# An FFT mix and a gated product on one core: split of the middle tiles behind two copies, one cast exempt from the hold, longer planned scalings, another order in the first batch

## The chip, the cores and the metric

The kernel runs on one core of a Trainium2 chip. The core has a matrix engine (TensorE, PE), a vector engine (VectorE, DVE), a scalar engine (ScalarE, ACT), a general engine (GpSimd, POOL) and a sync engine (SyncE, SP) that here only issues DMAs. Each works through its own instructions in the order in which the program wrote them, and waits on semaphores for the others. The metric is the device time of one execution in microseconds (us).

## The reference

```python
Xr, Xi = rfft(x, axis=1)                  # x: 8 x 3072 x 256, real
Yr = Xr @ w_r - Xi @ w_i + b_r            # complex linear layer, 256 x 256
Yi = Xr @ w_i + Xi @ w_r + b_i
Yr = sign(Yr) * max(abs(Yr) - 0.01, 0)    # soft shrinkage, Yi the same
y  = irfft(Yr + 1j * Yi, n=3072, axis=1)
out = (y @ w_a) * (y @ w_b) @ w_out       # w_a, w_b: 256 x 1536, w_out: 1536 x 256
```

All of it is float32. The kernel gets that from TensorE with three matmuls for each product: both operands are split in a high and a low part (`h` and `l` in the names), and high x low, high x high and low x high are summed in PSUM. Each split costs a cast (the high part) and a subtraction (the low one).

## The kernel before

**The stages.** The transform of a sequence (a batch, b, of 8) is done in pieces: `fdft` (a small network of adds on POOL and scalings on ACT over a buffer `fd`), f1 (a DFT matmul into `gst`, stored to DRAM as g_d, for the first batches), f2 (a middle DFT of one of 12 tiles u, whose result is split into `sx`), f3 (the complex linear layer and the shrinkage on `zy`, `zc`), i1 (back, into `dst`, stored as d_d), and `idft` (a network of adds on POOL and scalings on ACT over a buffer `wk`), which leaves `y`. y is split into `ych`, `ycl` by yr_split, after sums and differences of its parts (yr_sums).

**The loop.** The second half of the work, w_a, w_b and w_out, runs in 384 steps: 32 pairs p (four quarters q of each batch) times 12 column blocks j. A step (`step`, from L1484) issues seven products of three matmul groups each, by a scheme that saves products through sums. PSUM banks X (bank 3 and 4 in turn), ya (bank 5) and yb (bank 6) hold them. Three times a step ACT copies a bank to SBUF, `s` (L1492, function `take`): s1 after run 0, s2 after run 2, s5 after run 3. Run 2 needs s1 done, run 5 needs s2 and run 4 needs s5, since they go on in the same banks. At the step's end DVE adds and multiplies in yb, ACT casts the result to the high part `g` (L1554), and DVE subtracts for the low part; only then is yb free for run 3 of the next step. The products with w_out (`proj`) read g.

**The slots.** Twice a step, `slot()` takes a task from a list: one f1, f2, f3, i1 or part of the inverse transform of the next batch, so that the transform of batch b + 1 lies between the products of batch b. The list of a pair has 24 slots; `extra(work, n, f)` hangs f on slot n. Filler matmuls (`busy`) stand in front of the loop and keep PE going.

**The planner.** Class `Order` decides where in each engine's program an instruction stands. It holds a planned time for PE and the time until which each other engine is taken, and charges an instruction a fixed time and one for each element (`COST`). A chain of dependent operations is either urgent (its first operations go out by a heap as soon as their planned start is reached), or lazy (it goes out when its engine is planned to be free), or spare (lazier still). `od.hold` is a time: a lazy operation of ACT that would end later than it is not written yet, so that the next copy `s` isn't behind it. `od.need` and `od.vacate` force a chain out at once.

**What the change touches.** The g cast of a step is the first lazy operation after two urgent ones (`urgent=2`, L1554). The split of a middle tile (L945 to L977) is a chain of six operations: cast sx, copy xs, two on DVE, cast sx, one on POOL, of which four are urgent. The scalings are in idft (L1249) and fdft (L1337). `near_move` (L804) moves batch 0's g at the start and loads the first raw weights.

Of the kernel before, what the change touches and what calls it, by code (L numbers as in the profile page):

```python
# [12 lines left out]
F32 = mybir.dt.float32  # L13
# [4 lines left out]
B, S, D, DFF = 8, 3072, 256, 1536  # L18
# [4 lines left out]
M1, G = 24, 5  # L23
# [260 lines left out]
RING = 9  # L284
AHEAD = 1
LATE = 3
# [5 lines left out]
class Order:  # L292
# [34 lines left out]

    def chain(self, *ops, urgent=0, spare=False, after=0.0, hop=None):

        c = {"ops": deque(ops), "left": len(ops), "n": len(ops), "times": [(max(self.pe + self.FROM, after), None)], "urgent": urgent, "hop": self.HOP if hop is None else hop}
        if urgent:
            self._push(c)
        else:
            (self.spare if spare else self.lazy).append(c)
        return c
# [20 lines left out]
    def _held(self, c):  # L358

        if self.hold is None:  # L360
            return False
        e, t = self._choose(c)
        return e == "A" and t > self.hold
# [79 lines left out]
def fft_mix_glu_kernel(ctx: ExitStack, tc: tile.TileContext, x, w_r, w_i, b_r, b_i, w_a, w_b, w_out, c1f, vf, m2, t2, c3, b1, m2b, mf, vb, out):  # L443
# [360 lines left out]
    def near_move():  # L804
        g = state["g"]
        near_load(0, nc.sync.dma_start)
        near_load(1, nc.scalar.dma_start)
        for k in range(2):
            for i in range(2):
                r0 = 4 * (2 * k + i)  # L810
                dma = nc.scalar if k and i else nc.gpsimd
                dma.dma_start(gt[0, k][0][4 * NEAR :, i], g[r0 : r0 + 4])
        for h in range(2):
            n0 = NEAR + 4 * h
            nc.sync.dma_start(g_d[0][16:, n0 * D : (n0 + 4) * D], g[16:, 4 * h : 4 * h + 4].rearrange("p n d -> p (n d)"))
            if h == 0:
                state["wab_load"](1)
        raw = state["raw0"] = state["tmp"].tile([P, 2, 2 * FC], U32, tag="raw", name="wraw", bufs=3)
        for dh in range(2):
            nc.gpsimd.dma_start(raw[:, dh ^ 1], words[0][dh * P : (dh + 1) * P, : 2 * FC])  # L820
# [70 lines left out]
    def f2(b, u):  # L891
# [60 lines left out]
        else:  # L952
# [24 lines left out]
            ops[2:2] = [("G", 10, lambda e: nc.gpsimd.tensor_copy(both3[:, :, 0], xs_[:, :, 0]))]  # L977
        c = od.chain(*ops, urgent=4 if u else 1)
        od.reads(bk, c, 2 if u else len(ops) - 1)
# [240 lines left out]
    def idft(b, q, wait=False):  # L1220
# [25 lines left out]
        def scale(o, x, f):  # L1246
            n = size(*o[1:])
            o, x = at(*o), at(*x)
            ops.append(("A", n, lambda e: nc.scalar.mul(o, x, f)))  # L1249

# [59 lines left out]
    def fdft(b, q):  # L1310
# [23 lines left out]
        def scale(o, x, f):  # L1334
            n = size(*o[1:])
            o, x = at(*o), at(*x)
            ops.append(("A", n, lambda e: nc.scalar.mul(o, x, f)))  # L1337

# [9 lines left out]
    def yr_sums(p):  # L1348
        g = "GV" if p < NPAIR else "G"
        a11, a12, a21, a22 = yr["y"]  # L1350
# [20 lines left out]
    def yr_split(p, k, urgent=0):  # L1371
# [7 lines left out]
        l = state["ring"].tile([P, W], F32R, tag="ycl", name="ycl")  # L1379
        e = "V" if p == 0 else "GV" if p < NPAIR else "G"  # L1380
        ops = split(W, s, wide(h[:, :]), wide(l[:, :]), e)
# [92 lines left out]
    def step(n, nxt):  # L1474
# [46 lines left out]
        od.need(c1_)  # L1521
        od.hold = None
        run(2, X)
# [22 lines left out]
        if n:  # L1546
# [8 lines left out]
            ("V", W, lambda e: tt(e, l1, Y, h1.bitcast(F32), ALU.subtract)),  # L1555
            urgent=2,
        )
        od.reads(yb, c, 0)
# [9 lines left out]
    def first_mid_tasks():  # L1568
        ts = [lambda: f2(0, 0)]
        for u in range(14):  # L1570
# [8 lines left out]
            if u + 2 < 12:  # L1579
                ts.append(lambda u=u: f2(0, u + 2))  # L1580
        return ts

# [28 lines left out]
    with tc.manual_schedule():  # L1611
# [23 lines left out]
        ts[0] = after(ts[0], lambda: [od.put(xs[0, 0][2]), state.pop("start_weights")()])  # L1635
        ts[5] = after(ts[5], lambda: rest.append(split_mix()))

# [9 lines left out]
        ts[-3] = after(ts[-3], lambda: od.put(zs_done[11]))  # L1647
        ts[-2] = after(ts[-2], lambda: [od.put(rest[0]), busy(5, *unread), rows()])
        ts[-9] = after(ts[-9], matrices)
# [5 lines left out]
        have(DFF // FC - 1)  # L1655
        busy(20, *unread)
        for t in f1_tasks(1)[:AHEAD]:
# [46 lines left out]
        for b in range(B):  # L1704
            for q in range(NPAIR):
# [9 lines left out]
                if b == q == 0:  # L1715
# [8 lines left out]
                    extra(work, len(work) - 1, lambda: [mid_load(1, u) for u in range(2)])  # L1724
                    work.append(lambda: f2(1, 0))
                    mids = deque([None, None, *mid_tasks(1, 0)])
                elif b == 0 and q < 3:
                    n = 14 if q == 1 else 10
                    work = [mids.popleft() for _ in range(n)] + fin
                    work += [mids.popleft() for _ in range(20 - n)]  # L1730
                    for n, k in ((11, 1),) if q == 1 else ((3, 2), (19, 3)):
                        extra(work, n, lambda k=k: fdft(2, k))
                elif b + 1 < B:
# [3 lines left out]
                    if q < 3:  # L1737
                        if b + 2 < B:
                            extra(work, 13, lambda b=b, q=q: fdft(b + 2, q + 1))
                    else:  # L1740
                        extra(work, len(work) - 1, lambda b=b: idft(b + 1, 0, True))
                        if b + 2 < B:
                            extra(work, 13, lambda b=b: ahead(b + 2))
                            if b + 3 < B:
                                extra(work, 16, lambda b=b: fdft(b + 3, 0))
                            extra(work, 18 if b else 20, lambda b=b: f2(b + 2, 0))
# [45 lines left out]
```

## Time and profile before

| | us |
|---|---|
| median of 3 runs | 2759.38 (2756.68 to 2763.39) |
| the profiled execution | 2763.56 |
| its span | 2761.8 |
| TensorE busy | 2709.3 (98%), 16184 matmuls |
| ACT, DVE, POOL busy | 1474.5, 1854.8, 1626.7 (53%, 67%, 59%) |

The profile is of one execution. It is 4.2 us above the median of the three timed runs and 0.2 above the slowest of them. The 1.8 us between it and its span are ahead of the first and behind the last instruction. Several views are used below: the page's busy times; the waits, which say how long an engine was idle and whose instruction ended the idle time; timelines, where a line is an instruction or a row of equal ones, with the idle time of the engine ahead of it in brackets; and windows, the same stretch for all engines with TensorE's granted clock (1.00 is 2.4 GHz, 0.50 is 1.2 GHz).

### The profile page before, as it was taken

To read this page: it belongs to the slowest core of one execution; us is meant where nothing else is said; L and a number is where in the kernel's file an instruction comes from. 1 tells how busy PE (TensorE), PEld (TensorE's weight loads), DVE (VectorE), ACT (ScalarE), POOL (GpSimd) and SP (SyncE) were. 2 spreads that over 40 slices of the span, in tenths; PEclk is the share of its full clock that TensorE was granted. 3 is DMA by queue.
4 is the path that set the end of the run, shared out by engine and by line. 5 is a ranking of instruction groups with operands and counts; after the bars stand their busy time and mean duration, and the time that the engine had idled before them with its cause. 6 is when DMAs were issued, how large, how long until landed. Compare 5 with 4: busy or idle time off the path is not lost.

```text
span 2761.8 us, 44935 instructions
## 1 busy us (share of the span) xinstructions
PE 2709.3 (98%) x16184; PEld 2551.7 (92%) x16184; DVE 1854.8 (67%) x3541; ACT 1474.5 (53%) x3353; POOL 1626.7 (59%) x1818
## 2 busy tenths in 40 slices
PE   8999999999999999999999999999999999999999
PEld 5789998999999999999999999999999999999998
DVE  4776775666667666667666666666666666666666
ACT  4555554555555555555555555555555555555554
POOL 1125656776677767776767766676666543344440
PEclk9999999999999999999999999999999999999999
DMA  7542323232122322122321322213222122100000
GB/s 239 162 123 66 97 69 80 64 81 71 56 56 70 82 75 59 59 69 69 79 71 45 86 72 60 66 56 86 71 50 75 37 62 60 45 22 20 21 9 24
DMA packets 315910, 190.88 MB, mean 69 GB/s; under 512 B 230658, under 2 KB 291742, under 8 KB 315686
## 3 DMA queue, kind: packets, MB, share of 16 engines
q1 hardware_dynamic: 313498, 180.19, 23.8%
q0 software_dynamic: 1952, 7.58, 0.9%
q8 instruction: 127, 2.08, 0.3%
q14 instruction: 97, 0.79, 0.1%
q10 hardware_dynamic: 236, 0.23, 0.0%
HBM read 112.41 MB, written 75.42 MB: 68 GB/s over the span
## 4 chain that ended last, share of the span: by engine, by line
PE 84%; ACT 5%; POOL 5%; DVE 2%; DMA 2%; issue 1%; SPq 0%; ACTq 0%; POOLq 0%; DVEq 0%
PE bank L474 84%; POOL fd L468 2%; ACT fd L1337 1%; ACT s L1492 1%; DVE zy L468 1%; DMA g_f<-fd 1%; POOL ycl L468 1%; POOL y L468 1%; ACT zc L1107 1%; DVE bank L468 1%; DMA g_d<-gst 1%; ACT sx L945 1%; ACT wk L1249 0%; POOL s L468 0%; ACT g L1554 0%
## 5 line engine op out<-in xcount | busy, mean ns | idle before, releaser
L468 DVE TENSOR_TENSOR s<-bank,s 128x384 f32<-128x384 f32 x768 | 427.1, 556 | 502.3 <-PE bank L474 426.6
L468 DVE TENSOR_TENSOR bank<-bank,s 128x384 f32<-128x384 f32 x1152 | 648.1, 563 | 50.8 <-PE bank L474 14.6
L468 POOL TENSOR_TENSOR fd<-fd 128x192 f32<-128x192 f32 (+4 forms) x624 | 561.1, 909 | 193.0 <-ACT fd L1337 111.7
L468 POOL TENSOR_TENSOR wk<-wk 128x512 f32<-128x512 f32 (+4 forms) x532 | 520.1, 995 | 222.0 <-ACT wk L1249 158.0
L1492 ACT COPY s<-bank 128x384 f32<-128x384 f32 x1152 | 544.0, 487 | 185.2 <-PE bank L474 167.0
L1554 ACT CAST g<-bank 128x384 fp32r<-128x384 f32 x384 | 184.1, 479 | 763.5 <-DVE bank L468 473.5
L468 DVE TENSOR_TENSOR g<-bank,g 128x384 fp32r<-128x384 f32 x768 | 427.6, 557 | 220.8 <-ACT g L1554 198.4
L1467 ACT CAST g<-bank 128x384 fp32r<-128x384 f32 x384 | 186.3, 485 | 164.8 <-DVE bank L468 164.8
L474 PE MATMUL bank<-ych,wc3l 128*128 128x384 f32 x672 | 234.4, 349 | 19.0 <-ACT s L1492 18.4
L474 PE MATMUL bank<-ych,wc0l 128*128 128x384 f32 x672 | 233.5, 347 | 7.4 <-DVE g L468 4.2
L468 POOL TENSOR_TENSOR sx<-xq,sx 128x256 fp32r<-128x256 f32 x84 | 62.2, 740 | 297.7 <-ACT sx L949 293.9
L474 PE MATMUL bank<-ych,wc1l 128*128 128x384 f32 x672 | 231.0, 344 | 3.5 <-ACT s L1492 2.6
L474 PE MATMUL bank<-ych,wc2l 128*128 128x384 f32 x672 | 229.8, 342 | 2.1 <-DVE g L468 2.0
L474 PE MATMUL bank<-ycl,wc0h 128*128 128x384 f32 x672 | 226.4, 337 | 2.2 <-POOL ycl L468 2.2
L474 PE MATMUL bank<-ycl,wc3h 128*128 128x384 f32 x672 | 227.3, 338 | 0.0
L474 PE MATMUL bank<-ych,wc3h 128*128 128x384 f32 x672 | 227.3, 338 | 0.0
L474 PE MATMUL bank<-ycl,wc1h 128*128 128x384 f32 x672 | 226.2, 337 | 0.0
L474 PE MATMUL bank<-ycl,wc2h 128*128 128x384 f32 x672 | 226.2, 337 | 0.0
L474 PE MATMUL bank<-ych,wc0h 128*128 128x384 f32 x672 | 226.1, 336 | 0.0
L474 PE MATMUL bank<-ych,wc1h 128*128 128x384 f32 x672 | 226.1, 336 | 0.0
L474 PE MATMUL bank<-ych,wc2h 128*128 128x384 f32 x672 | 225.9, 336 | 0.0
L474 PE MATMUL bank<-wm_h,sx 128*128 128x256 f32 x1008 | 187.0, 281 | 0.0
(218 smaller groups left out, 6296.6 us busy)
## 6 DMA issues: line engine op xcount, KB each, us to landing
d_d<-dst SPq DMA_DIRECT2D x96, 256.0 KB
out_dram<-osb SPq DMA_DIRECT2D x64, 384.0 KB
wk<-d_d SPq DMA_DIRECT2D x28, 768.0 KB
fd<-in_x_dram SPq DMA_DIRECT2D x24, 768.0 KB
g_f<-fd SPq DMA_DIRECT2D x72, 256.0 KB
gt<-g_f SPq DMA_DIRECT2D x72, 256.0 KB
vt<-const_vb_dram SPq DMA_DIRECT2D x91, 128.0 KB
mf_in<-const_mf_dram SPq DMA_DIRECT2D x78, 128.0 KB
```

The costliest lines, as they stand in the source:

```text
L468: (nc.vector if e == "V" else nc.gpsimd).tensor_tensor(o, a, b, op=op)
L474: nc.tensor.matmul(o, lhsT=l, rhs=r, start=start, stop=stop, **kw)
L945: ("A", 512, lambda e: nc.scalar.copy(xh2, all_)),
L1107: ("A", 512, lambda e: nc.scalar.activation(z, y, AF.Relu, bias=state["lam"])),
L1337: ops.append(("A", n, lambda e: nc.scalar.mul(o, x, f)))
L1467: ("A", W, lambda e: nc.scalar.copy(h, X)),
L1492: return s, od.chain(("A", W, lambda e: nc.scalar.copy(s, q[:, :W])), urgent=1)
L1554: ("A", W, lambda e: nc.scalar.copy(h1, Y)),
```

## The change

The diff without blank lines and comments:

```diff
-AHEAD = 1
+AHEAD = 3
...
-    def chain(self, *ops, urgent=0, spare=False, after=0.0, hop=None):
-        c = {"ops": deque(ops), "left": len(ops), "n": len(ops), "times": [(max(self.pe + self.FROM, after), None)], "urgent": urgent, "hop": self.HOP if hop is None else hop}
+    def chain(self, *ops, urgent=0, spare=False, after=0.0, hop=None, free=False):
+        c = {"ops": deque(ops), "left": len(ops), "n": len(ops), "times": [(max(self.pe + self.FROM, after), None)], "urgent": urgent, "hop": self.HOP if hop is None else hop, "free": free}
...
     def _held(self, c):
-        if self.hold is None:
+        if self.hold is None or c["free"]:
             return False
...
+        x0 = p1.tile([P, 2, 2], F32, tag="x0", name="x0")
+        nc.gpsimd.tensor_copy(x0[:, 0, 0:1], gt[0, 0][0][:, 0, 0:1])
         raw = state["raw0"] = state["tmp"].tile([P, 2, 2 * FC], U32, tag="raw", name="wraw", bufs=3)
         for dh in range(2):
             nc.gpsimd.dma_start(raw[:, dh ^ 1], words[0][dh * P : (dh + 1) * P, : 2 * FC])
@@ f2: the split of a tile @@
-        c = od.chain(*ops, urgent=4 if u else 1)
+        c = od.chain(*ops, urgent=0 if u else 1)
@@ idft, and the same in fdft @@
-            ops.append(("A", n, lambda e: nc.scalar.mul(o, x, f)))
+            ops.append(("A", n + 170, lambda e: nc.scalar.mul(o, x, f)))
@@ yr_sums @@
-        g = "GV" if p < NPAIR else "G"
+        g = "GV" if p <= NPAIR else "G"
@@ yr_split @@
-        e = "V" if p == 0 else "GV" if p < NPAIR else "G"
+        e = "V" if p == 0 else "GV" if p <= NPAIR else "G"
@@ step @@
         od.need(c1_)
-        od.hold = None
+        od.hold = od.pe + 3 * (W / 2.4 + 2.8) + od.FROM - 250.0
         run(2, X)
...
             ("A", W, lambda e: nc.scalar.copy(h1, Y)),
             ("V", W, lambda e: tt(e, l1, Y, h1.bitcast(F32), ALU.subtract)),
             urgent=2,
+            free=True,
@@ first_mid_tasks @@
+        ts[4:6] = ts[5:3:-1]
...
-        ts[5] = after(ts[5], lambda: rest.append(split_mix()))
+        ts[6] = after(ts[6], lambda: rest.append(split_mix()))
-        ts[-2] = after(ts[-2], lambda: [od.put(rest[0]), busy(5, *unread), rows()])
+        ts[-2] = after(ts[-2], lambda: [od.put(rest[0]), rows(), busy(5, *unread)])
-        busy(20, *unread)
+        busy(8, *unread)
         for t in f1_tasks(1)[:AHEAD]:
             t()
@@ the lists of slots, b == 0 and q == 0 first @@
-                    work.append(lambda: f2(1, 0))
-                    mids = deque([None, None, *mid_tasks(1, 0)])
+                    extra(work, 20, lambda: f2(1, 0))
+                    mids = deque(mid_tasks(1, 0))
                 elif b == 0 and q < 3:
-                    n = 14 if q == 1 else 10
-                    work = [mids.popleft() for _ in range(n)] + fin
-                    work += [mids.popleft() for _ in range(20 - n)]
-                    for n, k in ((11, 1),) if q == 1 else ((3, 2), (19, 3)):
+                    work = [mids.popleft() for _ in range(12)] + fin
+                    work += [mids.popleft() for _ in range(8)]
+                    for n, k in ((14, 1),) if q == 1 else ((5, 2), (20, 3)):
                         extra(work, n, lambda k=k: fdft(2, k))
...
-                        if b + 2 < B:
+                        if b == 1 and q == 0:
+                            extra(work, 1, lambda: fdft(3, 0))
+                            extra(work, 19, lambda: fdft(3, 1))
+                        elif b + 2 < B:
                             extra(work, 13, lambda b=b, q=q: fdft(b + 2, q + 1))
...
-                            if b + 3 < B:
+                            if 0 < b < B - 3:
                                 extra(work, 16, lambda b=b: fdft(b + 3, 0))
```

So: the six operations of a middle tile's split become lazy; the chain that holds the g cast is never held; a scaling is planned as if it had 170 elements more; a second hold lies ahead of the copy s2. At the start the first raw weight loads wait, by way of a copy of one element on POOL, for gt[0,0]; f3(0,1,0) stands ahead of f2(0,2); three f1 of batch 1 stand ahead of the loop in place of one, and 8 filler matmuls in place of 20. In batch 0 the list of slots is laid out anew, and fdft(3,0) goes from the last pair of batch 0 to the first of batch 1. Sums and splits of pair 4 may be planned on DVE as well as on POOL.

ACT, step 154 of the loop (in batch 3; in the trace before at 1222 to 1227 us), from its first copy `s` on, before (bank3, bank4: X; bank6: yb; bank7: the bank of the slots; L1467 casts a product's other g):

```order
L1492 COPY s_12626<-bank3_72 128x384
L1107 ACTIVATE zc_12613<-zy_12611,lam_113 128x512
L1337 ACTIVATE fd_12379<-fd_12379 128x192 x2
L1467 CAST g_12596<-bank4_73 128x384
L1337 ACTIVATE fd_12379<-fd_12379 128x192
L945 CAST sx_12651<-bank7_76 128x2x256
L946 COPY xs_12653<-bank7_76 128x256
L1492 COPY s_12661<-bank3_72 128x384
L1492 COPY s_12667<-bank6_75 128x384
```

The same place after:

```order
L1494 COPY s_12613<-bank3_72 128x384
L1109 ACTIVATE zc_12601<-zy_12599,lam_113 128x512
L1469 CAST g_12583<-bank4_73 128x384
L947 CAST sx_12639<-bank7_76 128x2x256
L1494 COPY s_12646<-bank3_72 128x384
L1494 COPY s_12653<-bank6_75 128x384
L948 COPY xs_12641<-bank7_76 128x256
L1339 ACTIVATE fd_12369<-fd_12369 128x192 x2
```

Before, three scalings of `fd` and the copy xs stand ahead of the last two copies `s`; after, they stand behind them, and zc, the cast of g and the cast sx are left ahead.

DVE, steps 145 and 146 (in the trace before at 1163 to 1168 us), before; `g<-bank6` is the low part of g, which frees yb, and `s<-bank5,s` the sum of s1 and ya:

```order
L468 TENSOR_TENSOR bank6_75<-bank6_75,s_11960 128x384
L468 TENSOR_TENSOR bank6_75<-bank6_75,s_11925 128x384
L468 TENSOR_TENSOR bank4_73<-bank4_73,s_11966 128x384
L468 TENSOR_TENSOR s_12007<-bank5_74,s_12007 128x384
L468 TENSOR_TENSOR g_11988<-bank6_75,g_11987 128x384
L468 TENSOR_TENSOR g_11988<-bank4_73,g_11987 128x384
L468 TENSOR_TENSOR s_12033<-bank3_72,s_12033 128x384
L468 TENSOR_TENSOR bank6_75<-bank6_75,s_12024 128x384
```

After:

```order
L468 TENSOR_TENSOR bank6_75<-bank6_75,s_11948 128x384
L468 TENSOR_TENSOR bank6_75<-bank6_75,s_11913 128x384
L468 TENSOR_TENSOR g_11978<-bank6_75,g_11977 128x384
L468 TENSOR_TENSOR bank4_73<-bank4_73,s_11957 128x384
L468 TENSOR_TENSOR s_11995<-bank5_74,s_11995 128x384
L468 TENSOR_TENSOR g_11978<-bank4_73,g_11977 128x384
L468 TENSOR_TENSOR s_12019<-bank3_72,s_12019 128x384
```

The subtraction `g` out of bank 6 was behind `s<-bank5` and is ahead of it now.

ACT in front of the loop (in the trace before at 104 to 117 us), with what each instruction waits for; `gst` is f1's output on its way to g_d, `y` the first pair's:

```order
L578 ACTIVATE w_t_753<-wraw_601 128x768 [waits DMASW3_49,DMASW2_49]
L465 COPY gst_784<-bank4_73 120x512 [waits DMAHW1_49,PE_49,Activation_49]
L465 COPY y_827<-bank5_74 128x12x32 [waits DVE_49,PE_49,Activation_49]
L465 COPY y_827<-bank6_75 128x12x32 [waits PE_49]
L594 CAST ych_833<-y_827 128x384 [waits Activation_49]
L594 CAST ych_836<-y_827 128x384 [waits Activation_49]
L465 COPY y_827<-bank7_76 128x12x32 [waits PE_49]
L465 COPY y_827<-bank1_70 128x12x32 [waits PE_49]
```

After:

```order
L578 ACTIVATE w_t_755<-wraw_603 128x768 [waits DMASW3_49,DMASW2_49]
L465 COPY gst_774<-bank4_73 120x512 [waits DMAHW3_49,PE_49,Activation_49]
L465 COPY gst_779<-bank5_74 120x512 [waits DVE_49,DMAHW4_49,PE_49,Activation_49]
L465 COPY gst_786<-bank6_75 120x512 [waits DMAHW3_49,PE_49,Activation_49]
L465 COPY y_830<-bank7_76 128x12x32 [waits DVE_49,PE_49]
L465 COPY y_830<-bank1_70 128x12x32 [waits PE_49]
L594 CAST ych_836<-y_830 128x384 [waits Activation_49]
L594 CAST ych_839<-y_830 128x384 [waits Activation_49]
L465 COPY y_830<-bank2_71 128x12x32 [waits PE_49]
```

Three copies `gst` stand ahead of the first copy `y`, where one stood; the third waits for a DMA queue of its own besides PE.

## Rows read from the trace of the kernel before

**Rows 1.** The page's first part: busy us, share, instructions of each engine

```profile
PE 2709.3 (98%) x16184; PEld 2551.7 (92%) x16184; DVE 1854.8 (67%) x3541; ACT 1474.5 (53%) x3353; POOL 1626.7 (59%) x1818
```

**Rows 2.** PE's waits, whole span: total us, times, longest us

```profile
PE bank L474 <- DMA gt<-g_d: 4.3, 2, 2.7
...
PE bank L474 <- DMA m_in<-const_m_dram: 2.7, 1, 2.7
...
PE bank L474 <- DMA wk<-d_d: 2.4, 1, 2.4
```

**Rows 3.** PE's waits from 495 us to the end

```profile
PE bank L474 <- ACT s L1492: 15.4, 26, 2.6
...
PE bank L474 <- DVE g L468: 6.2, 10, 0.7
```

**Rows 4.** Timeline, ACT, 1224 to 1227: start us, us, line, operation [idle before]

```profile
1224.47 0.76 ACT L1337 ACTIVATE fd<-fd 128x192 f32<-128x192 f32 x2 [0.88 <-POOL fd L468]
...
1225.14 0.46 ACT L1467 CAST g<-bank 128x384 fp32r<-128x384 f32 x1
...
1225.50 0.37 ACT L1337 ACTIVATE fd<-fd 128x192 f32<-128x192 f32 x1
...
1225.77 0.58 ACT L945 CAST sx<-bank 128x512 fp32r<-128x512 f32 x1
...
1226.23 0.38 ACT L946 COPY xs<-bank 128x256 f32<-128x256 f32 x1
...
1226.49 0.88 ACT L1492 COPY s<-bank 128x384 f32<-128x384 f32 x2
```

**Rows 5.** Timeline, PE, 1225.5 to 1227.1

```profile
1225.58 0.40 PE L474 MATMUL bank<-g,wo9h 128*128 128x256 f32 x2
1227.05 0.44 PE L474 MATMUL bank<-ych,wc3l 128*128 128x384 f32 x1 [1.07 <-ACT s L1492]
```

**Rows 6.** Timeline, DVE, at 1167

```profile
1166.98 0.55 DVE L468 TENSOR_TENSOR g<-bank,g 128x384 fp32r<-128x384 f32 x1
```

**Rows 7.** Timeline, PE, 1166.6 to 1167.6

```profile
1166.67 0.34 PE L474 MATMUL bank<-ycl,wc0h 128*128 128x384 f32 x1
...
1167.58 0.44 PE L474 MATMUL bank<-ych,wc0l 128*128 128x384 f32 x1 [0.57 <-DVE g L468]
```

**Rows 8.** Windows: us, busy of PE, PEld, DVE, ACT, POOL, granted clock, DMA

```profile
113.40:120.30 6.90, 6.90 (x26) 5.88 (x25) 3.97 (x8) 3.66 (x8) 0.00 (x0) 0.51 0.48 131
...
1891.70:1895.30 3.60, 3.60 (x11) 3.23 (x11) 2.17 (x5) 1.43 (x5) 2.53 (x5) 0.53 0.00 0
```

**Rows 9.** PE's waits from 130 to 470 us

```profile
PE bank L474 <- ACT s L1492: 2.5, 5, 1.2
```

**Rows 10.** PE's waits from 470 to 495 us

```profile
PE bank L474 <- ACT s L1492: 6.2, 2, 4.7
...
PE bank L474 <- POOL ycl L468: 2.2, 2, 1.4
```

**Rows 11.** Timeline, POOL, 455 to 476

```profile
455.76 4.88 POOL L468 TENSOR_TENSOR fd<-fd 128x768 f32<-128x768 f32 x3
...
475.93 3.85 POOL L468 TENSOR_TENSOR y<-wk 128x384 f32<-128x384 f32 x4
```

**Rows 12.** Timeline, all engines, 103 to 113

```profile
103.06 5.14 PE L474 MATMUL bank<-wm_h 128*128 128x512 f32 x20
...
104.32 0.38 SPq L1134 DMA_DIRECT2D d_d<-dst  x1
...
108.05 1.02 PE L474 MATMUL bank<-xin,fk 120*120 120x512 f32 x2
...
109.12 0.70 SPq L1176 DMA_DIRECT2D wk<-d_d  x2
...
111.30 0.36 SPq L833 DMA_DIRECT2D g_d<-gst  x1
...
112.69 0.48 ACT L465 COPY y<-bank 128x384 f32<-128x384 f32 x1 [2.96 <-PE bank L474]
```

More of the change, by code (lines that the diff above doesn't have):

```diff
@@ L1336, in scale @@
             o, x = at(*o), at(*x)
-            ops.append(("A", n, lambda e: nc.scalar.mul(o, x, f)))
+            ops.append(("A", n + 170, lambda e: nc.scalar.mul(o, x, f)))
         _network(op(ALU.add), op(ALU.subtract), scale)
```

## The prediction

> **What bounds the kernel now.** I read the page's busy shares first: TensorE (PE) is busy for 98% of the span, ScalarE (ACT) for 53%, GpSimd (POOL) for 59% [rows 1]. So an edit is worth only what it takes from PE's idle time, from PE's time at half clock, or from PE's own work. Next I read PE's waits, for the whole run and then by stretch. At the start PE waits for loads: gt 4.3 us, m_in 2.7, wk 2.4 [rows 2]. From 495 us to the end it waits 26 times for the copy `s` at L1492, 15.4 us together, and 10 times for `g` from VectorE (DVE), 6.2 us [rows 3]. Last I read timelines round single waits; one of each name stands for its kind.
>
> The first kind is one at 1226 us [rows 4, 5]. PE issued two matmuls at 1225.58, about 0.12 apart, and could go on at 1225.82. It went on at 1227.05, 1.23 late, of which the view calls 1.07 idle. ACT ran late: two scalings of `fd` waited 0.88 for POOL, and since ACT works in its written order the cast of `g`, a third scaling, the cast sx, the copy xs and only then the two copies `s` followed. PE needs the first of these copies (run 5 of the step needs s2).
>
> The second kind is one at 1167 us [rows 6, 7]. PE issues a matmul every 0.17, so 1166.84 was due after 1166.67; it came at 1167.58, 0.74 late, of which 0.57 is called idle. It needed the bank yb, which the subtraction `g` frees at 1167.53; on DVE that subtraction stands behind another `s`, because the cast of g had been put late.
>
> Both times the loss is 0.16 more than the idle shown. The 36 waits of rows 3 are then 15.4 + 6.2 + 36 x 0.16 = 27.4 us. One of them, 2.6 long, is followed by a stretch of 3.6 us at a granted clock of 0.53, so nearly all of it at 1.2 in place of 2.4 GHz [rows 8]: half of 3.4 us is lost, 1.7. Together 29.1.
>
> **The change, part by part.**
>
> *Split of middle tiles lazy, cast of g never held, scalings planned longer, second hold.* These rewrite ACT's order in every step of the loop and are one sum. In the first order fence the third scaling and xs go behind the copies, and so do the two scalings on which ACT waited 0.88. Between the first copy `s` and the next two remain zc, the cast of g and sx. By the starts in rows 4, gone are 0.67 + 0.27 + 0.26 of work and the wait of 0.88, 2.08 against a loss of 1.23: this stall goes. Late next are the xs copy itself and DVE's sum that reads it, by the two copies' length, about 0.7. Their reader is an f3 in a later slot with other matmuls between; where that cover is missing it costs up to 0.5 a tile (rival three).
>
> The planner charged 215 ns for a scaling of 192 elements (58 + 0.82 x 192); two took 0.76, so 0.38 each [rows 4]. With 354 it puts fewer in front of a copy `s`. The second order fence shows the other kind: g is now written ahead of `s`. Counted over DVE's whole order, g stands behind that `s` in 11 steps before and in 6 after, of which the first stands ahead of 495 us in both: 10 go, 5 come. The price of a cast that is never held is an ACT instruction ahead of a copy `s` where none stood. In some 18 steps (those in which a product's output tile is copied too) the cast now stands ahead of the second copy and xs behind it: 0.36 in, 0.26 out [rows 4], 0.1 each, 1.8 at most. Sum of this part: 29.1 - 5 x 0.74 - 1.8 = 23.6 gained. Its ends: twice the new late places (7.4) and 0.26 for each of the 18 (4.7), 17 gained; or nothing given back, 29.
>
> *130 to 470 us, first batch.* PE waits 2.5 in five waits for `s` [rows 9]; with 0.16 each, 3.3. The tables put fdft one to three slots later and f2(1,0) earlier. I take 2.5 gained, as most of the same kind goes elsewhere; ends 0 and 3.3.
>
> *470 to 495 us, where batch 1 takes over.* PE waits 6.2 and 2.2 in four waits [rows 10]; with 0.16 each 9.0, and behind the one of 4.7 I add the half clock that rows 8 show behind one of 2.6, another 1.7: 10.7. The cause is POOL: `fd` work of 4.88 us at 455.76 stands between the `wk` steps of the inverse transform, so that its last step, `y`, starts at 475.93 only [rows 11]. Afterwards that fdft starts in the next pair, the inverse transform a step (7 us) sooner, and sums and splits of pair 4 may run on DVE. That could cover all of it; but two scalings of wk still gather ahead of one copy `s` there. I take half, 5.5 gained, ends 2 and 10.
>
> The Trainium skill speaks against one piece of this: "GPSIMD Engine Reference", section "1. Specifications", says that GpSimd shares its SBUF interfaces with VectorE, with contention where a DVE instruction has two SBUF inputs, as those sums have. No row shows how much. If POOL stood still during ten such instructions as long as the one in rows 6, this part's gain would be nothing.
>
> *Start.* The first raw weight loads go out behind gt[0,0], so they move no bytes while PE waits 4.3 for gt [rows 2]; and f3(0,1,0) goes ahead of f2(0,2), the step that waits 2.7 for m_in. I take 3 gained. Ends: 0, if the later raw weights make their own readers late by as much; 7.0, if both waits go.
>
> *AHEAD 3, busy 8.* Two more f1 stand ahead of the loop, 2 x 1.02 [rows 12], and the same leaves the slots: nothing. Twelve filler matmuls go, 20 of which took 5.14, so 3.1 [rows 12]; PE then waits for wk in their place, 1 longer than the 2.4. Against it stands the third order fence: three copies gst are ahead of the y copies, where one was. The tile has two buffers, so the third waits until the first store to g_d has landed. That store was issued at 111.30 [rows 12]; a further pair of xin loads now goes ahead of it. How long it flies is not shown; a load that waits for the store of 104.32 went out at 109.12, so 4.8 at most [rows 12], at least nothing. The y copies, at 112.69 before, then come between 112.7 and 117.5. I take 116: the first product loses 3.3, and the two f1 gone from the slots give about 1.3 each back, with what they make late there. I book 0.7 lost; ends 4 lost and 2 gained.
>
> Round this place stands a stretch of 6.9 us at a granted clock of 0.51, behind PE's idle 2.4 [rows 2, 8]. The Trainium skill ("TensorE: Matmul & The Clock Gate", section "Loop structure matters more than you think") says that long DMA waits between matmuls let PE go cold; the trace agrees. By it a wait made 1 longer by the missing fillers would cost such a stretch, 3.4, once more.
>
> **Sum.** 23.6 + 2.5 + 5.5 + 3 - 0.7 = 33.9 less than the profiled execution's 2763.6: 2729.7. That execution is 4.2 above the median of the runs, 2759.4. The wait of 2.6 with its half clock costs 4.5 where its fellow in rows 5 costs 1.23; I take the 3.2 between them for its own, so 30.7 from the median, 2728.7. Losses too short to be listed as waits should shrink as well; I say 2727.
>
> **Rivals.** *One, the waits move.* ACT has as much to do as before; what stands no longer ahead of one copy stands ahead of the next: scalings two steps on, ych of the next pair. For it: 26 of the 36 waits are ACT's. Against it: ACT is idle for 47% [rows 1]. Half of the sum would stay: 2763.6 - 17 = 2746.
>
> *Two, it does not show.* ACT's lateness in rows 4 begins with POOL (0.88), and the change makes POOL no faster. If the scalings land in front of a copy all the same, only the start and the place at 470 gain, 8, and the wait of the third gst takes 4: 2760.
>
> *Three, slower.* The split of a middle tile ends too late for its f3. Each of 77 tiles has xs behind two copies, and if the slack behind it is under 0.2 of the 0.7, PE loses 0.5 a tile: 77 x 0.5 = 38 against 34 gained, 2768. Against it: no wait of PE for sx is among those of rows 3.
>
> **How the numbers follow.** Forecast 0.70, rival one 0.16, two 0.07, three 0.07. All low ends together are 17 + 0 + 2 + 0 - 4 = 15 gained, all high ones 29 + 3.3 + 10 + 7 + 2 = 51; as they seldom fall together, the forecast's own range is 24 to 46, 2717 to 2740. The range for 8 in 10 reaches to rival one: 2714 to 2747. A change under 0.2% (5.5 us) can't be told from none. Faster by more: the forecast, rival one and a piece of two, 0.88; within it 0.07; slower 0.05.
>
> **What the profile after would show.** Right: PE's waits for `s` from 495 us on fall from 26 to under 10, those for `g` from 10 to about 5; near 1226 the copies `s` start right behind sx; the wait near 475 is under 3 us; no half clock behind 495. Wrong: a new name among PE's waits (sx, ych) with more than 10 us in all, a first product well behind 119, or a half clock round 111 much longer than 6.9 us.

## The result and the profile after

The changed kernel takes 2729.15 us (median of 4 runs, 2728.12 to 2729.76), the kernel before 2759.94 beside it; the ratio is 0.9888 (95% interval 0.9871 to 0.9905). The forecast was 2727, and the profiled execution (span 2726.3) is the one of 2728.12. The total came out as forecast, though its terms did not: by the two profiles the loop behind 495 us gained 6 us more than booked, the start 4 more (most of it because the kernel before began late in its profile, as shown below), and the first batch with the handover to the next 9 less.

The page's busy line, after; TensorE's busy time fell by 12.6 us against [rows 1], the span by 35.5:

```profile
PE 2696.7 (99%) x16172; PEld 2549.6 (94%) x16172; DVE 1853.2 (68%) x3554; ACT 1473.1 (54%) x3353; POOL 1620.9 (59%) x1806
```

PE's waits, whole span, after (us in total, times, longest us):

```profile
PE bank L474 <- DVE g L468: 7.2, 1, 7.2
PE bank L474 <- ACT s L1494: 6.7, 5, 2.7
PE bank L474 <- DMA gt<-g_d: 3.0, 2, 2.6
PE bank L474 <- ACT y L465: 2.3, 1, 2.3
PE bank L474 <- ACT ych L594: 1.7, 1, 1.7
```

And from 495 us to the end, where [rows 3] had 36 waits:

```profile
PE bank L474 <- ACT s L1494: 1.7, 2, 1.3
PE bank L474 <- ACT g L1469: 0.2, 1, 0.2
```

The 26 waits for `s` are 2, the 10 for `g` on DVE none. At step 154, the first kind of stall [rows 4, 5], ACT now runs like this (timeline; L1494 was L1492, L1339 was L1337):

```profile
1207.47 0.48 ACT L1494 COPY s<-bank 128x384 f32<-128x384 f32 x1 [0.22 <-PE bank L474]
...
1209.08 0.48 ACT L1469 CAST g<-bank 128x384 fp32r<-128x384 f32 x1 [0.34 <-DVE bank L468]
1209.46 0.59 ACT L947 CAST sx<-bank 128x512 fp32r<-128x512 f32 x1
1210.00 0.94 ACT L1494 COPY s<-bank 128x384 f32<-128x384 f32 x2
1210.84 0.38 ACT L948 COPY xs<-bank 128x256 f32<-128x256 f32 x1
1211.10 0.78 ACT L1339 ACTIVATE fd<-fd 128x192 f32<-128x192 f32 x2
```

And PE beside it:

```profile
1210.74 0.40 PE L474 MATMUL bank<-g,wo9h 128*128 128x256 f32 x2
1210.97 0.34 PE L474 MATMUL bank<-ych,wc3l 128*128 128x384 f32 x1
```

The first of the two copies `s` (they overlap; one takes 0.48) is written by 1210.5, and PE starts run 5 at 1210.97 without idle time: half a microsecond of slack where 1.07 us were idle. xs and the scalings of `fd` stand behind the copies.

The rest of the gain and loss is found by setting the first copy `s` of some steps side by side, since every step does the same work in both kernels. Start of step 1: 124.80 before, 118.05 after. From there to step 46: 338.47 and 340.58. From 46 to 50, where batch 1 takes over: 38.93 and 37.72. From 50 to the last step, 383: 2246.36 and 2216.76. So between these two profiles the start gained 6.8, the first batch lost 2.1, the handover gained 1.2 and the rest 29.6. The 6.8 is mostly the spread of the start: step 1 begins between 117.2 and 124.8 us in the five profiled kernels with the old start (the kernel before is the latest of them) and between 118.1 and 121.7 in the six with the changed start and AHEAD 3.

New or longer waits stand in four places between 104 and 480 us. Three are shown here; the fourth, for `ych` in step 35 (1.7), comes up again with fd20. ACT, in front of the loop, after (timeline), and PE behind it:

```profile
106.24 0.58 ACT L465 COPY gst<-bank 120x512 f32<-120x512 f32 x1 [5.65 <-DMA g_d<-gst]
106.72 0.87 ACT L465 COPY y<-bank 128x384 f32<-128x384 f32 x2
```

```profile
109.22 0.69 PE L474 MATMUL bank<-ych,wc0l 128*128 128x384 f32 x1 [2.27 <-ACT y L465]
```

The third `gst` stood 5.65 us for the first store to g_d, as the prediction said it would, and with it the y copies, for which PE waited 2.27. From 103.8 to 114.2, round that wait, the granted clock was 0.51: 10.4 us near half clock, where [rows 8] have 6.9. Next, DVE, POOL, PE and ACT at steps 9 and 10, after (timeline, all engines):

```profile
175.40 5.92 POOL L468 TENSOR_TENSOR fd<-fd 128x768 f32<-128x768 f32 x4
...
178.43 0.88 DVE L583 TENSOR_SCALAR wo_a<-wo_a 128x256 f32<-128x256 f32 x1 [0.16 <-ACT wo_a L578]
...
179.34 1.05 DVE L584 TENSOR_SCALAR wo_a<-wo_a 128x256 uint32<-128x256 uint32 x1
...
180.42 1.19 DVE L585 SCALAR_TENSOR_TENSOR wo_a<-wo_raw,wo_a 128x256 uint32<-128x256 uint32 x1
...
183.41 0.45 PE L474 MATMUL bank<-ych,wc3l 128*128 128x384 f32 x1 [1.82 <-ACT s L1494]
...
191.97 0.40 ACT L594 CAST wo11h<-wo_b 128x256 fp32r<-128x256 f32 x1 [2.26 <-DVE wo_b L468]
...
193.30 0.69 PE L474 MATMUL bank<-ych,wc3l 128*128 128x384 f32 x1 [2.72 <-ACT s L1494]
```

`fd`, with adds of 768 elements, runs on POOL from 175.40 to 181.32; beside it three DVE instructions that decode w_out take 0.88, 1.05 and 1.19. In the kernel before, the same three instructions (DVE, timeline) had no POOL work beside them:

```profile
183.57 0.28 DVE L583 TENSOR_SCALAR wo_a<-wo_a 128x256 f32<-128x256 f32 x1
183.89 0.29 DVE L584 TENSOR_SCALAR wo_a<-wo_a 128x256 uint32<-128x256 uint32 x1
...
185.94 0.41 DVE L585 SCALAR_TENSOR_TENSOR wo_a<-wo_raw,wo_a 128x256 uint32<-128x256 uint32 x1
```

After, PE waits 1.82 and then 2.72 for the copies behind them, and the matmul at 193.30 takes 0.69 because it runs at half clock: from 193.4 to 198.0 the granted clock was 0.50. Last, DVE at the handover, after, and PE behind it:

```profile
470.22 0.56 DVE L468 TENSOR_TENSOR s<-y 128x384 f32<-128x384 f32 x1 [5.81 <-POOL y L468]
...
471.89 0.56 DVE L468 TENSOR_TENSOR bank<-bank,s 128x384 f32<-128x384 f32 x1
```

```profile
473.89 0.69 PE L474 MATMUL bank<-ych,wc3l 128*128 128x384 f32 x1 [7.18 <-DVE g L468]
```

The three sums of pair 4 that now stand on DVE (470.22 to 471.89) waited 5.81 for POOL's `y`, and DVE's own work for step 47 stood behind them: 7.18 us of idle PE in one wait, in place of the 6.2 and 2.2 in four waits of [rows 10].

Of the forecast's signs, those behind 495 us came out as right: 2 waits for `s` and none for `g` on DVE, the copies right behind sx, no half clock there. Two others did not: the wait near 475 is 7.18 in place of under 3, and the half clock in front of the loop grew from 6.9 to 10.4.

### The profile page after: what moved, and what is told of

Read it like the earlier page. It is cut to its first block, busy times and chain, and to the rows that moved or that the text cites. A ratio compares the mean times of both kernels' runs of the same rounds, so it can differ in the third digit from the quotient of the medians.

```text
span 2726.3 us, 44938 instructions
## 1 busy us (share of the span) xinstructions
PE 2696.7 (99%) x16172; PEld 2549.6 (94%) x16172; DVE 1853.2 (68%) x3554; ACT 1473.1 (54%) x3353; POOL 1620.9 (59%) x1806
## 4 chain that ended last, share of the span: by engine, by line
PE 96%; DVE 1%; DMA 1%; ACT 1%; issue 0%; POOL 0%; SPq 0%; ACTq 0%; DVEq 0%; POOLq 0%
PE bank L474 96%; DMA xin<-in_x_dram 0%; DVE bank L468 0%; DMA g_d<-gst 0%; DVE s L468 0%; ACT s L1494 0%; DMA gt<-g_d 0%; DMA fk<-in_x_dram 0%; POOL y L468 0%; ACT g L1556 0%; DMA vt<-const_vb_dram 0%; ACT ych L594 0%; DVE wo_b L468 0%; DVE g L468 0%; ACT y L465 0%
## 5 line engine op out<-in xcount | busy, mean ns | idle before, releaser
L1494 ACT COPY s<-bank 128x384 f32<-128x384 f32 x1152 | 547.4, 485 | 165.3 <-PE bank L474 149.4
```

The lines of the kernel that those rows point to most:

```text
L1494: return s, od.chain(("A", W, lambda e: nc.scalar.copy(s, q[:, :W])), urgent=1)
```

## The experiments

Kernels timed together share the runs of the kernel before; between such groups its median moved from 2757.8 to 2760.8, so ratios are compared, and 0.001 is 2.8 us. Each interval is about 0.0015 to either side.

**Which edits make the gain behind 495 us?** Four kernels made from the one before: all four planner edits; and three of them one at a time. (`free=True` comes with the argument `free` of `chain` and its test in `_held`, as in the change.)

```diff
@@ free_only (and in four) @@
             urgent=2,
+            free=True,
@@ lazy_only (and in four) @@
-        c = od.chain(*ops, urgent=4 if u else 1)
+        c = od.chain(*ops, urgent=0 if u else 1)
@@ scale_only, twice (and in four) @@
-            ops.append(("A", n, lambda e: nc.scalar.mul(o, x, f)))
+            ops.append(("A", n + 170, lambda e: nc.scalar.mul(o, x, f)))
@@ four @@
-        od.hold = None
+        od.hold = od.pe + 3 * (W / 2.4 + 2.8) + od.FROM - 250.0
         run(2, X)
```

> The kernel before with the four edits of the steady loop alone (free g cast, lazy split of middle tiles, scalings planned longer, second hold); start, first batch's slots and pair 4 as before. Theory A, that the gain behind 495 us is these edits' alone: 26 to 30 us less than before, about 2731, and the waits for s and g behind 495 us fall from 36 to under 5; the place at 470 us stays at 8 to 10 us of waits. Rival B, that the new start and the new slots of batch 0 shift the later work into place: under 15 us less, and over 15 of the 36 waits stay.

> The kernel before with the g cast never held, nothing else. In DVE's order no g stands behind the next s any more (10 did behind 495 us), and scalings ahead of the second copy s fall from 52 to 42 steps, while xs stays ahead of it in 70. Theory A (each kind of wait has its own cause: the held cast makes the g waits; xs and scalings ahead of the copies make the s waits): the 10 waits for g go, 7.8 us, a few of the 26 for s as well: 8 to 12 us less, about 2750. Rival B (the scalings' planned price is the one cause of both): under 4 us less.

> The kernel before with the split of middle tiles lazy, nothing else. xs stands ahead of the second copy s in 5 steps in place of 70, scalings in 42 in place of 52, late g's behind 495 us are 4 in place of 10. Theory A: most of the waits for s go, 15 us, and 6 of the late g's, 4 us: about 19 less, 2740. Rival B (planned price of the scalings): the scalings stay ahead of the copies, under 8 us less.

> The kernel before with the scalings planned 170 elements longer, nothing else. xs stays ahead of the second copy in 70 steps, scalings in 55, and late g's behind 495 us rise from 10 to 16 by the order. Theory A: the waits for g cost 4 us more and the waits for s stay or lose a few: between 5 less and 5 more than before, about 2758. Rival B (the planned price is what matters): 15 us less or more.

| kernel | us | ratio (95%) |
|---|---|---|
| four | 2727.01 | 0.9892 (0.9877 to 0.9907) |
| free_only | 2743.28 | 0.9946 (0.9931 to 0.9961) |
| lazy_only | 2741.14 | 0.9935 (0.9921 to 0.9950) |
| scale_only | 2736.70 | 0.9925 (0.9909 to 0.9942) |

The waits from 495 us on, of four, free_only, lazy_only and scale_only in turn:

```profile
PE bank L474 <- ACT s L1492: 0.5, 1, 0.5
```

```profile
PE bank L474 <- ACT s L1492: 9.7, 25, 0.9
```

```profile
PE bank L474 <- ACT s L1492: 3.6, 7, 0.6
PE bank L474 <- DVE g L468: 2.6, 4, 0.7
```

```profile
PE bank L474 <- DVE g L468: 4.0, 6, 0.7
PE bank L474 <- ACT s L1492: 1.5, 5, 0.3
```

The four edits alone give the whole gain (theory A of the first; 0.9892 against 0.9888 for the whole change). The single ones give 14.5, 16.6 and 21.1 us, 52 together where all four give 31: they overlap. Theory A of the other three, a cause for each kind of wait, holds in part: free_only removes every wait for g, lazy_only leaves 4 of them and few for s. But free_only gains more than the 8 to 12 of theory A, and with scale_only theory A fails and rival B, 15 us or more, holds: the order still shows 16 late g's and xs ahead of the copies in 70 steps, and yet only 6 waits for g and 1.5 us for s are left.

The shared part stands in the traces. In the kernel before, 5 of the 26 waits for `s`, half of their time (7.5 of 15.4 us), come in steps 58, 106, 154, 202 and 250, where two scalings of `fd` wait for POOL ahead of the copies, as in [rows 4]. In all three single kernels these two stand behind the copies in all five steps, and at most 0.33 us of wait for the second copy is left in any of them. Step 154 in free_only (ACT, timeline):

```profile
1219.06 0.89 ACT L1492 COPY s<-bank 128x384 f32<-128x384 f32 x2
1220.26 0.76 ACT L1337 ACTIVATE fd<-fd 128x192 f32<-128x192 f32 x2 [0.30 <-POOL fd L468]
```

Ahead of the other 21 waits for `s` (0.22 to 0.47 each) ACT did not wait for POOL. free_only leaves all of these, lazy_only the six in steps with copies of an output tile, scale_only one. How each edit brings this about inside the planner is argued from its code, not shown.

**Which of them can go again?** From the changed kernel, without the longer price, and without the second hold.

```diff
@@ un_scale, twice @@
-            ops.append(("A", n + 170, lambda e: nc.scalar.mul(o, x, f)))
+            ops.append(("A", n, lambda e: nc.scalar.mul(o, x, f)))
@@ un_hold @@
-        od.hold = od.pe + 3 * (W / 2.4 + 2.8) + od.FROM - 250.0
+        od.hold = None
         run(2, X)
```

> The changed kernel with the scalings planned as before. Scalings stand ahead of the second copy in 47 steps in place of 57, no late g's behind 495 us, 4 or more scalings ahead of the first copy in 35 steps in place of 46. Theory A (what scale_only gained, lazy split and free cast gain as well, so the edits overlap): within 2 of the changed kernel. Rival B (the planned price carries most of the gain): 8 or more above it.

> The changed kernel without the second hold. By the order scalings stand ahead of the second copy s in 66 steps in place of 57, late g's are 1 behind 130 us in place of 5. Theory A (lateness comes from work between the copies): some waits for s return, 2 to 6 more than the changed kernel. Rival B (the other three leave enough slack): within 1.5 of it.

un_scale: 2737.84, ratio 0.9918 (0.9903 to 0.9933), 8 us above the changed kernel: the 8 of rival B, though 8 of 30 is not most of the gain. Its waits from 495 us on:

```profile
PE bank L474 <- ACT s L1494: 4.6, 11, 0.6
```

Seven of these, 0.56 each, come in steps with copies of an output tile (`osb`), where the cast of g now stands ahead of the second copy; in step 73 two scalings of `fd` stand ahead of the first copy as well, and in the changed kernel, where they do not, there is no wait. From step 50 to 383 un_scale needs 7.4 us more. un_hold: 2732.31, ratio 0.9899 (0.9884 to 0.9914), which overlaps 0.9888. From step 50 to 383 it needs 0.3 more, and two waits for s are listed:

```profile
PE bank L474 <- ACT s L1494: 1.2, 2, 0.7
```

So its 3 us, if they are any, are not from waits there; in its profile step 1 begins at 120.65 in place of 118.05, within the spread of the start. Rival B as far as the trace shows, unsettled by the time.

**What happens in the first batch?** From the changed kernel: fdft(2,0) on slot 20; pair 4 on POOL; AHEAD 1 with its 20 fillers; the first two together.

```diff
@@ fd20 (and in best_b) @@
-                    extra(work, len(work) - 3, lambda: fdft(2, 0))
+                    extra(work, 20, lambda: fdft(2, 0))
@@ pool4 (and in best_b) @@
-        g = "GV" if p <= NPAIR else "G"
+        g = "GV" if p < NPAIR else "G"
-        e = "V" if p == 0 else "GV" if p <= NPAIR else "G"
+        e = "V" if p == 0 else "GV" if p < NPAIR else "G"
@@ ahead1 @@
-AHEAD = 3
+AHEAD = 1
-        busy(8, *unread)
+        busy(20, *unread)
-                    extra(work, 20, lambda: f2(1, 0))
+                    extra(work, 22, lambda: f2(1, 0))
```

> The changed kernel with fdft(2,0) hung on slot 20 of the first pair in place of slot 15 (where the list that is two f1 shorter had put it; slot 17 in the kernel before). Theory A, that the two waits of 1.8 and 2.7 us at 181 and 190 us come from its 768-wide adds on POOL running beside DVE's decoding of w_out: the decoding instructions at L583 to L585 take 0.3, 0.3 and 0.4 again in place of 0.9, 1.1 and 1.2, both waits and the half clock behind the second go, 4 to 6 us less than the changed kernel, about 2724. Rival B, that ACT's order at the new slots makes them: the decoding gets faster, yet one wait of 2 us or more stays there, under 2.5 us less.

> The changed kernel with sums and splits of pair 4 on POOL alone again. Theory A, that the wait of 7.2 us at 474 comes from three sums on DVE that wait for POOL's y ahead of DVE's own work for step 47: that wait falls to 2 to 4, and waits for ycl of 1 to 2 come behind it: 2 to 4 us less than the changed kernel, 2726. Rival B, that PE waits for y itself, whichever engine sums: no less, up to 2 more since a sum takes 1.0 on POOL and 0.56 on DVE.

> The changed kernel with AHEAD 1 and 20 filler matmuls as before (f2(1,0) on slot 22, since f1 ends later). Theory A, that the third f1 in front of the loop costs the wait for the copy y (2.3) and, by a list two slots shorter, the waits at 181 and 190: these three go, 2.4 of f1 come back into slots: about 4 less than the changed kernel, 2725. Rival B, that three f1 ahead and fewer fillers are worth what they cost: 2 us more.

> The changed kernel with both, fdft(2,0) on slot 20 and pair 4 on POOL alone. By theory A of both the gains add: 6 to 9 less than the changed kernel, 2721; by the rivals under 3 less.

| kernel | us | ratio (95%) |
|---|---|---|
| fd20 | 2725.61 | 0.9879 (0.9864 to 0.9893) |
| pool4 | 2725.54 | 0.9876 (0.9861 to 0.9891) |
| ahead1 | 2723.60 | 0.9870 (0.9855 to 0.9884) |
| best_b | 2722.45 | 0.9865 (0.9849 to 0.9882) |

All four medians lie within 2 us of what theory A said, though fd20's gain (0.0009, 2.5 us) is under its 4 to 6; and each interval overlaps the changed kernel's (0.9871 to 0.9905), so the traces decide. fd20, DVE's decoding, POOL beside it and PE (timeline, all engines):

```profile
181.74 1.01 POOL L468 TENSOR_TENSOR s<-y 128x384 f32<-128x384 f32 x1 [2.70 <-ACT y L465]
...
182.03 0.87 DVE L583 TENSOR_SCALAR wo_a<-wo_a 128x256 f32<-128x256 f32 x1 [0.15 <-ACT wo_a L578]
...
182.94 0.29 DVE L584 TENSOR_SCALAR wo_a<-wo_a 128x256 uint32<-128x256 uint32 x1
...
183.26 0.42 DVE L585 SCALAR_TENSOR_TENSOR wo_a<-wo_raw,wo_a 128x256 uint32<-128x256 uint32 x1
...
185.49 0.44 PE L474 MATMUL bank<-ych,wc3l 128*128 128x384 f32 x1 [0.30 <-ACT s L1494]
...
193.69 0.44 PE L474 MATMUL bank<-ych,wc3l 128*128 128x384 f32 x1 [1.26 <-ACT s L1494]
```

The decoding takes 0.29 and 0.42 again, but for the one at 182.03, beside another POOL sum, and PE's waits are 0.30 and 1.26 in place of 1.82 and 2.72; of the second, what is left goes with ACT's order, in which the cast wo11h, fed by DVE, stands ahead of the copies in step 10 (so rival B holds for that part). From step 8 to step 12 it needs 29.5 us, the changed kernel 34.8. Behind it the wait for ych in step 35, 1.7 in the changed kernel, has grown to 2.5 with a half clock after it, and takes 2.2 of that back. pool4, PE at the handover (timeline):

```profile
471.84 0.44 PE L474 MATMUL bank<-ych,wc3l 128*128 128x384 f32 x1 [2.15 <-ACT s L1494]
...
477.20 0.44 PE L474 MATMUL bank<-ycl,wc0h 128*128 128x384 f32 x1 [2.31 <-POOL ycl L468]
```

Two waits in place of one of 7.18; from step 46 to 50 it needs 34.7, the changed kernel 37.7. In ahead1 the wait for the y copies is gone (ycl, 0.7, is what PE waits for between 104 and 130 us), and steps 8 to 12 take 29.3. The half clock in front of the loop is gone too: from 100 to 125 us the granted clock was 1.00, where the changed kernel has 0.80.

**The start, and a version that beats both.** best_c is ahead1 with pair 4 on POOL; best_c_start takes the start's part out of it.

```diff
@@ best_c_start against best_c @@
-        x0 = p1.tile([P, 2, 2], F32, tag="x0", name="x0")
-        nc.gpsimd.tensor_copy(x0[:, 0, 0:1], gt[0, 0][0][:, 0, 0:1])
-        ts[4:6] = ts[5:3:-1]
-        ts[6] = after(ts[6], lambda: rest.append(split_mix()))
+        ts[5] = after(ts[5], lambda: rest.append(split_mix()))
-        ts[-2] = after(ts[-2], lambda: [od.put(rest[0]), rows(), busy(5, *unread)])
+        ts[-2] = after(ts[-2], lambda: [od.put(rest[0]), busy(5, *unread), rows()])
```

> The changed kernel with AHEAD 1 and 20 fillers (f2(1,0) on slot 22) and with pair 4 on POOL alone. If the gains of ahead1 and pool4 add: 8 to 10 less than the changed kernel, about 1.4 to 1.5% under the kernel before, 2720; if the waits only trade places, as ahead1, 2724.

> best_c without the start's part of the change: the raw weight loads are not held for gt[0,0], f2(0,2) stands ahead of f3(0,1,0), the fillers ahead of the rows as before. Theory A, that these are worth what the waits of the first 104 us in the kernel before suggested: 2 to 4 more than best_c. Rival B, that the start of the kernel before was late in its profile by chance (loop begins at 117.9 us, at 111.2 to 114.4 in four kernels with the same start): within 1.5 of best_c.

best_c: 2720.00, ratio 0.9853 (0.9838 to 0.9868), an interval that ends below the changed kernel's (0.9871). best_c_start: 2724.56, ratio 0.9870 (0.9854 to 0.9887), 4.6 us more: theory A, and a little above its range. The two intervals overlap by 0.0014, but all four times of the one lie above all four of the other. Waits of the first 104 us, best_c and then best_c_start:

```profile
PE bank L474 <- DMA gt<-gst: 0.8, 1, 0.8
PE bank L474 <- DMA gt<-g_d: 0.8, 1, 0.8
...
PE bank L474 <- DMA m_in<-const_m_dram: 0.2, 1, 0.2
```

```profile
PE bank L474 <- DMA gt<-g_d: 2.8, 2, 1.5
PE bank L474 <- DMA m_in<-const_m_dram: 1.3, 1, 1.3
```

Behind 104 us best_c_start waits 2.0 for wk, and from 100 to 125 us its granted clock was 0.80; best_c has no such wait, and 1.00. These are one profile each, and the start spreads: with the same start, step 0 begins at 117.9 us in the kernel before and at 111.2 to 114.4 in the first four kernels above. The medians carry the verdict here, the waits and the clock agree with it. The 4.6 hold with AHEAD 1 and 20 fillers; with AHEAD 3, as changed, the start shows no gain beyond its spread.

At the handover best_c needs 33.75 us from step 46 to 50, 5.2 less than the kernel before.

## Why the prediction was right, point by point

**The planner's edits, 23.6 booked, 31 found.** four gained 30.8 in time, and the changed kernel 29.6 from step 50 on, a little above the upper end of 29. The mechanism was right, and the 29.1 of idle and half clock that the rows showed were the right size. Wrong were the terms given back, "5 x 0.74" for late g's and 1.8 for the steps with an output copy, where the changed kernel has no wait. Behind 495 us the g's are late in DVE's order in steps 122, 170, 218 and 266 (the fifth that was counted, step 47, lies ahead of 495 us, at the handover), and no wait for g is listed in these four. Step 170, after, shows why (PE, then DVE, timeline):

```profile
1322.27 1.05 PE L474 MATMUL bank<-vt,zh 128*128 128x128 f32 x8
1323.08 0.42 PE L474 MATMUL bank<-ych,wc0l 128*128 128x384 f32 x1
...
1323.69 0.37 PE L474 MATMUL bank<-ych,wc0l 128*128 128x384 f32 x1
```

```profile
1323.01 1.01 DVE L468 TENSOR_TENSOR g<-bank,g 128x384 fp32r<-128x384 f32 x2
```

A slot's eight matmuls stand at 1322.27 ahead of run 2, so run 3, which needs yb, comes at 1323.69, when the first of the two subtractions that start at 1323.01 (0.55 each) is over; in step 146 before, no slot stood between runs 0 to 3, and run 3 waited [rows 7]. Run 2 began there right behind run 1 (PE, before, timeline):

```profile
1166.23 0.43 PE L474 MATMUL bank<-ych,wc0l 128*128 128x384 f32 x1
```

scale_only says the same: of its 16 late g's only 6 cost a wait. A place in the order is not a wait: what PE does up to the need decides, and I had counted places.

**130 to 470 us, 2.5 gained booked, 2.1 lost.** AHEAD's shorter list moved fdft(2,0) two slots forward, onto the decoding of w_out: by the profiles steps 8 to 12 lost 5.4. Step 35, with its new wait for ych, lost 2.8. The other steps gained 6.1, in part because two f1 had left their slots. The prediction listed what AHEAD puts in front of the loop and what it takes from the slots, and said of the slots only "the same leaves", not that what follows them moves up.

**470 to 495 us, 5.5 booked, 1.2 found.** POOL's chain did end sooner, y at 470.2. But with the sums on DVE, DVE stood still for y too. That was the part that I had called cover ("sums and splits of pair 4 may run on DVE"); without it the place gives 4.2 (pool4) to 5.2 (best_c). The rule of the Trainium skill that I set against this part ("GPSIMD Engine Reference", section "1. Specifications") is about SBUF interfaces shared with GpSimd. The loss came by order, not by them: POOL was idle from 470.2 to 472.0, while the sums ran.

**The start, 3 booked, 4.6 measured** (best_c against best_c_start, with AHEAD 1). In the changed kernel nothing of it is left that stands out of the spread of the start, and the price of AHEAD 3 and of the missing fillers, next, may have taken it back.

**AHEAD and the fillers, 0.7 lost booked.** The third gst waited for its store as forecast, 3.2 us behind the store's issue, and PE 2.3 us for y. The wait for wk, booked 1 longer than 2.4, was 1.0; but the half clock came all the same, 10.4 us of it, where ahead1 and best_c have none. With the moved fdft the loss is the 5 us between the changed kernel and ahead1 (ratios 0.9888 and 0.9870; intervals overlap) or the 6 between pool4 and best_c (0.9876 and 0.9853; they overlap too).

Sum by the measured terms: 31 for the planner's edits and 4.6 for the start are won, 5 to 6 are lost by AHEAD and 3 to 4 by pair 4. That leaves 26 to 28 where 31 were measured; the 3 to 5 between may be the slots' new lists, which no run has alone, or noise. So the four planner edits are the gain, and the rest of the change adds nothing that can be told from none. That the sum came within 2 us of the forecast was luck: two terms that were too low made up for three that were too high. Rival one (the waits move) did happen, in the first batch above all; behind 495 us one such wait is new, 1.3 us in step 60. Rival three did not: none of PE's waits is for sx behind 495 us.

What stays open: what the second hold and the slots' new lists are worth, and which of the start's pieces (raw loads held, f3 ahead of f2, fillers behind the rows) gives the 4.6; they were not run apart.

## What to carry to other kernels

In an engine that works in written order, an instruction that waits for a slower engine must not stand in front of one that the bottleneck needs; three different edits gave 14.5 to 21.1 of the 31 us each, and all three moved the same few scalings back. When a step loses tasks from a list of slots, look at what moves up with it, and against which engine it then runs. Count a late place in an order as a loss only if the bottleneck reaches the need before it is met.

## What the runs showed of the hardware

DVE's decoding instructions, which read and write SBUF only, slowed threefold beside POOL's adds (0.88, 1.05 and 1.19 against 0.28, 0.29 and 0.41), and in fd20 the one at 182.03 took 0.87 and ended 0.15 behind the POOL sum of 181.74, while its successor at 182.94 took 0.29. DVE instructions that read a PSUM bank kept their 0.55 to 0.57 beside POOL work [rows 6]; POOL was busy for 2.92 of the 3 us from 1166 on. The whole trace of the kernel before agrees: `zh<-zy,zc`, which reads SBUF twice, took 0.68 in the median without POOL work beside it (63 times) and 0.83 with POOL beside it for over 0.3 of its time (21 times), while `bank<-bank,s` took 0.57 either way (319 and 795 times). The Trainium skill ("GPSIMD Engine Reference", section "1. Specifications") says that the two engines share SBUF interfaces, with contention where a DVE instruction runs in a 2-port mode or has two SBUF inputs. That fits L585 and `zh`, which have two; in which mode the ones at L583 and L584, with one input, ran, no trace here shows.
